# Own orders at the start and the end of a fused agent-attention and maxout kernel

## The chip, the cores and the metric

The kernel runs on one core of a Trainium2 chip. The metric is the device time of one execution in microseconds (us); less is better. The engines are TensorE (PE: matmuls and transposes), VectorE (DVE), ScalarE (ACT), GpSimd (POOL) and SyncE (SP), which issues the loads and stores.

## The reference

Two layers, one behind the other. `B, N, C = 4, 12544, 128`, 49 agents, 768 hidden features.

```python
def _attn_ref(q, k, v, agents):
    scale = 1.0 / np.sqrt(q.shape[-1])
    def sm(a, b):
        s = scale * (a @ b.transpose(0, 2, 1))
        s = s - s.max(-1, keepdims=True)
        e = np.exp(s)
        return e / (e.sum(-1, keepdims=True) + 1e-09)
    a2k = sm(agents, k)
    agent_v = a2k @ v
    q2a = sm(q, agents)
    return (q2a @ agent_v).astype(np.float32)

def _moe_ref(x, w1, w2, w3, w_out):            # x: the 50176 rows of the attention
    h = np.maximum(np.maximum(x @ w1, x @ w2), x @ w3)
    return (h @ w_out).astype(np.float32)
```

All inputs and the output are float32.

## The kernel before

The kernel never forms the attention's output. For each batch it reduces keys and values to a small matrix `avT` (agent values, 128 x 49), multiplies that with the difference of the weights (`wall`: w2-w1, w3-w1, and a linear part) into `G` (49 rows), and then each row of queries needs only its 49 exponentials `e` times `G`.

**Two kinds of groups.** A *key group* (`k_group`) covers 9 tiles of 128 rows: load, cast to bf16, transpose, scores against the agents, exponentials, values, add. Batch 0 is reduced by "early" key groups before any query; their rows are cut into ten groups of 9 tiles and two of 4, so the last one covers tiles 94 to 97. Batches 1 to 3 are reduced inside the query groups of the batch before. A *query group* (`q_group`, 49 of them, `s` = 0 to 48, 8 tiles each) loads and casts queries, transposes them on PE or by DMA, and makes scores and exponentials (`s`, `ex`). Then, for each of six slices `f` of the hidden features:

- `u<f>`: PE, the first hidden product (L533, two matmuls), into a PSUM tile of the ring "uv"
- `a<f>`: ScalarE, relu of it into SBUF (L548); for `f` = 3 in place (L545)
- `v<f>`: PE, the second hidden product (L533), into another tile of the ring "uv"; for `f` = 3 added to u3's tile
- `x<f>`: VectorE, the maximum of both into `r` (L558); for `f` = 3 ScalarE's relu (L556)
- `oc<o><f>`: PE, the output product of slice `f` for output half `o` (L572, four matmuls), added to the tile that `lin<o>` (L563) began
- `sc<o>`: scaling of output half `o` with the reciprocal row sums (L579); then one store of the group by SP

`sums` (PE, L521) and `rec` (VectorE, L527) make those reciprocals.

**Order by keys.** Every step is put down with `at(key, fn, name, needs, ring, frees)`, and `emit` sorts all steps by their key. A step whose `needs` have not been emitted, or whose PSUM ring has no free place, waits in a list and is emitted as soon as it can be. The rings are "uv" (3 tiles of two banks), "om" (2 tiles) and "a" (3 SBUF tiles of relu results). The emitted order is the order of each engine's own queue: each engine works strictly through it. `table(s)` chooses the keys of a query group: `KEY` for most, `BEGIN` and `BORDER` where a batch begins or is about to, `LATE` from group 36 on, the last batch, in which no keys are left to reduce.

**The seam.** `last_key` is the key of the last early key group. Around it stand that group's steps, the first query group's load, cast (POOL, L481), transposes (PE, L486), copy (ScalarE, L494), scores (L507) and exponentials, and the tail of batch 0's reduction (`k_tail`): `normalise` (L402, L403) makes `avT`, `product` (L421) multiplies it with `wall` in PSUM, and VectorE copies it into `G` (L426). For batch 0, `product` fills one "uv" tile in two parts, each copied out before the next begins, and then a second tile. All loads go through SP's queue into a ring of 14 SBUF tiles `st`; the early values are cast by ScalarE (L285), all keys and queries by POOL (L280, L481). Between the steps `keep_busy` puts a few matmuls without use (L254).

Of the kernel before, what the change touches and what calls it, by code (L numbers as in the profile page):

```python
# [16 lines left out]
def kernel(  # L17
# [78 lines left out]
        "oc11": 11.381, "oc13": 11.497,  # L96
    }
    PRODUCT_KEYS = (-8.717, -1.818)
    BEHIND = 2.6

    def table(s):
        if s + 1 in tails:
            return BORDER
        return BEGIN if s in tails and s < SB else KEY if s < SB else LATE
# [6 lines left out]
    def uv_tile(dtype=FP32):  # L111
        return psum.tile([P, 2, 512 if dtype == FP32 else 1024], dtype, tag="uv", bufs=3, name="uv_ps")
# [6 lines left out]
    def at(key, fn, name=None, needs=(), ring=None, frees=()):  # L119

        ops.append((key, len(ops), fn, name, needs, ring, frees))
# [61 lines left out]
    def load_tile():  # L185
        return loads.tile([P, KT, C], FP32, tag="st", name="st")
# [77 lines left out]
    def k_group(b, t0, n, key, s):  # L264
# [4 lines left out]
        if s == 0:  # L269
            key += BEHIND  # L270

        def load():
            for name, src in (("k", k), ("v", v)):
                t = d[name] = load_tile()
                nc.sync.dma_start(t[:, :n, :], src[b, t0 * P:(t0 + n) * P, :].rearrange(
                    "(p j) c -> p j c", j=n))
# [4 lines left out]

        def cast_v():
            d["vb"] = work.tile([P, KT, C], BF16, tag="v_bf", bufs=4, name="v_bf")
            if early:
                nc.scalar.activation(d["vb"][:, :n, :], d["v"][:, :n, :], AF.Copy)  # L285
            else:
                nc.gpsimd.tensor_copy(out=d["vb"][:, :n, :], in_=d["v"][:, :n, :])  # L287
# [59 lines left out]

        if early:
            g = ("early", t0)
            at(key - 30, load)  # L350
            at(key - 5, cast_k)
            at(key - 4, cast_v)
            at(key, turn_k, ("kt", g), (), "uv", [("kt_out", g)])
            at(key + 0.5, evacuate, ("kt_out", g), [("kt", g)])

            last = [("normalise", 0)] if t0 + n == NT else []
            late = max(0, (key - last_key) / 6 + 2)
            at(min(key + 6.6, last_key + 0.58 + 0.02 * late), scores, ("ks", g), [("kt_out", g)],
               "uv", [("ka", g)] + last)
            at(min(key + 7, last_key + 0.64 + 0.01 * late), exps, ("ke", g), [("ks", g)])  # L360
            done = last_key + (0.6 + 0.1 * late if late >= 1 else 0.55)
            at(min(key + 13.2, done), values, ("kv", g), [("ke", g)])
            at(min(key + 13.6, done + 0.01), add_values, ("ka", g), [("kv", g)])
        else:

            at(max(6.0 * s - 24.6, 6.0 * s - 21.05 if s in (4, 5) else -99), load)
            at(max(6.0 * s - 12.6, last_key - 3.4 + 0.2 * s), cast_k, ("k_cast", s))
            at(max(6.0 * s - 10.6, last_key - 3.3 + 0.2 * s), cast_v, ("v_cast", s))
            if s > 1:
                at(max(key - 9.1, last_key - 3.2), turn_k, ("kt_out", s), [("k_cast", s)])  # L370
            else:

                turn = 2.7 if s else last_key + 1.05
                at(turn, turn_k, ("kt", s), (), "uv", [("kt_out", s)])
                at(turn + 0.05, evacuate, ("kt_out", s), [("kt", s)])
            at(key + K["ks"], scores, ("ks", s), [("kt_out", s), ("ho", s)])
            at(key + K["ke"], exps, ("ke", s), [("ks", s)])
            at(key + K["ke"] + 1.5, add_exps, ("kx", s), [("ke", s)])
            at(key + K["kv"], values, ("kv", s), [("ke", s), ("v_cast", s)])
            at(key + K["ka"], add_values, ("ka", s), [("kv", s)])  # L380

    def k_tail(b, sum_key, keys, s):
        d = {}

        def reduce():
            w = KT // 2 * A
            t = Eacc[b]
            while w >= A:
                nc.gpsimd.tensor_tensor(out=t[:, :w], in0=t[:, :w], in1=t[:, w:2 * w], op=ALU.add)
                w = w // A // 2 * A  # L390
            nc.gpsimd.tensor_tensor(out=e_sum[:, :A], in0=t[:, :A], in1=t[:, KT * A - A:], op=ALU.add)

        def total():
            for h in range(2):
                nc.tensor.matmul(host[s][h * H:(h + 1) * H, :1], e_sum, ones[:, :1], start=True,
                                 stop=True, skip_group_check=True)

        def normalise():
            if s is None:

                r = last_tile["t"][:, :A]
                nc.vector.reciprocal(r, Vacc[b][:, A:])  # L402
                nc.vector.tensor_tensor(out=avT[:, b, :A], in0=Vacc[b][:, :A], in1=r, op=ALU.mult)  # L403
            else:
                nc.vector.reciprocal(r_ag[:, b:b + 1], host[s][:, :1])
            G[b] = work.tile([P, WC], BF16, tag="G", name="G")

        def product(c0, *ends):

            t = uv_tile().rearrange("p i c -> p (i c)")  # L410

            at0 = c0 if len(ends) == 1 else ends[0] - 512
            a = c0
            for z in ends:
                cuts = sorted({a, z} | {c for c in (at0 + 512, C1O) if a < c < z})
                for lo, hi in zip(cuts, cuts[1:]):
                    for h in range(2):


                        c = lo + (C if lo >= C1O and h == 0 else 0)  # L420
                        nc.tensor.matmul(t[h * H:(h + 1) * H, lo - at0:hi - at0], avT[:, b, :],  # L421
                                         wall[:, c:c + hi - lo], start=True, stop=True,
                                         skip_group_check=True)
                src = t[:, a - at0:z - at0]
                if s is None:
                    nc.vector.tensor_copy(out=G[b][:, a:z], in_=src)  # L426
                else:
                    nc.scalar.activation(G[b][:, a:z], src, AF.Copy, scale=r_ag[:, b:b + 1])
                a = z

        if s is not None:
            at(6.0 * (s - 1) + table(s - 1)["ke"] + 1.51, reduce, ("sum_e", b), [("kx", s - 1)])
            at(sum_key + 0.8, total, ("total", s), [("sum_e", b), ("ho", s)])
        at(sum_key + 0.81, normalise, ("normalise", b),
           [("ka", ("early", NT - last_size))] if s is None else [("total", s), ("ka", s - 1)])

        pieces = ((C31, C31 + 2 * P, C1O) if s is None else (C31, WC), (C21, C31))
        for i, piece in enumerate(pieces):
            at(keys[i], lambda piece=piece: product(*piece),
               ("product", b, i), [("normalise", b)], "uv", [("product", b, i)])  # L440


    def split(t0, t1, step):
# [10 lines left out]
    def q_group(s):  # L454
# [120 lines left out]
        def out_scale(o):  # L575
            if "out" not in d:
                d["out"] = work.tile([P, GT, C], FP32, tag="o_sb", bufs=3, name="o_sb")
            j, m = 2 * pairs[o][0], 2 * len(pairs[o])
            nc.vector.tensor_tensor(  # L579
                out=d["out"][:, j:j + m, :],  # L580
                in0=d["o", o].rearrange("p (j c) -> p j c", c=C),
                in1=d["r"][:, j:j + m].unsqueeze(2).to_broadcast([P, m, C]), op=ALU.mult)
# [14 lines left out]
        if s == 0:  # L597
            at(last_key - 29.9, load)
            at(last_key - 3.5, cast)
            at(last_key + 0.802, turn_q, ("qt", 0), (), "om", [("qe", 0)])  # L600
            at(last_key + 0.803, evacuate, ("qe", 0), [("qt", 0)])
            at(last_key + 0.94, scores, ("s", 0), [("qe", 0)], "om", [("ex", 0)])
            at(last_key + 0.941, exps, ("ex", 0), [("s", 0)])
        elif not q_dma:
            at(key - (21.08 if s in (4, 5) else 26), load)
            at(max(key - 12.8, last_key - 3.45 + 0.2 * s), cast, ("q_cast", s))
            put("qt", turn_q, ("q_cast", s), ring="om", frees=[("qe", s)])
            put("qe", evacuate, ("qt", s), *([("s", s - 3)] if s >= 3 else []))
        else:
            at(key - 32, load)  # L610
            at(key - 14.3, cast)
            at(key - 12.3, turn_q_dma, ("qe", s))
# [56 lines left out]
    for g, n in enumerate(first_sizes):  # L669
        k_group(0, sum(first_sizes[:g]), n, first_key + 6.0 * g, None)  # L670

        if 4 <= g < len(first_sizes) - 3:
            fillers += [(first_key + 6.0 * g + 0.55, 3), (first_key + 6.0 * g + 1.3, 3)]
    k_tail(0, last_key, (last_key + 0.95, last_key + 1.02), None)
    for key, n in fillers + [(last_key + 0.9, 2), (KEY["u1"] + 0.01, 2),
                             (KEY["u3"] + 0.05, 2)]:
        at(key, lambda n=n: keep_busy(n), ("busy", key), (), "om", [("busy", key)])
# [45 lines left out]
```

## Time and profile before

| | |
|---|---|
| time, median of 6 runs | 463.16 us (463.10 to 463.39) |
| the profiled execution's own time | 463.25 us |
| its span in the profile | 461.4 us, 13320 instructions |
| PE busy | 436.8 us (95%) |
| DVE busy | 402.3 us (87%) |
| ACT busy | 396.7 us (86%) |
| POOL busy | 171.4 us (37%) |
| DMA | 118.53 MB, mean 257 GB/s |
| granted TensorE clock | 1.00 |

The span runs from the first to the last instruction of the program; 1.85 us of the execution lie outside it. All times below are microseconds from the span's start. A busy share is a mean over stages that have different limits: until about 45 us the core mostly loads and reduces batch 0, then come 49 query groups, and behind the last one the output is scaled and stored. `DVE r L558` means an instruction of VectorE at line 558 of the kernel that writes the tile `r`.

### The profile page before, as it was taken

The page shows a single profiled execution, that of the slowest core. Times are in us where ns is not written, and L with a number is a line of the kernel's source. Part 1 is how long each engine was busy: PE and PEld are TensorE (multiplying, and loading weights), DVE is VectorE, ACT ScalarE, POOL GpSimd, SP SyncE. Part 2 cuts the span into 40 slices and gives each one's busy share as a digit, 9 for nine tenths or more (in the row PEclk, how much of TensorE's full clock was granted, in tenths as well). Part 3 has the DMA queues.
Part 4 walks back from the last instruction along what each step waited for, and adds up shares of the span by engine and source line. Part 5 has one row for each costly group of instructions (what it writes and reads, how often), then busy time and mean ns, then how long its engine had stood idle before and what let it go on. Part 6 is the DMA issues. An engine that isn't in the chain of part 4 may idle for free.

```text
span 461.4 us, 13320 instructions
## 1 busy us (share of the span) xinstructions
PE 436.8 (95%) x5457; PEld 273.9 (59%) x5462; DVE 402.3 (87%) x510; ACT 396.7 (86%) x460; POOL 171.4 (37%) x179
## 2 busy tenths in 40 slices
PE   2598899999999999999999999999999999999996
PEld 2465466666656666666666666666656555555554
DVE  3255899999989999999989999999988999999995
ACT  3365989999899899898998998999999999999982
POOL 2234964644462535445273355363240101100000
PEclk9999999999999999999999999999999999999999
DMA  8999999999998999987998999996766465644122
GB/s 316 408 409 391 352 325 353 333 345 263 312 305 284 305 267 342 283 268 246 301 317 277 280 316 304 284 266 188 162 149 183 127 195 151 180 118 125 60 94 91
DMA packets 82632, 118.53 MB, mean 257 GB/s; under 512 B 56391, under 2 KB 57867, under 8 KB 82571
## 3 DMA queue, kind: packets, MB, share of 16 engines
q1 hardware_dynamic: 82368, 117.59, 84.4%
q8 instruction: 42, 0.69, 0.6%
q14 instruction: 19, 0.16, 0.1%
q10 hardware_dynamic: 203, 0.10, 0.1%
HBM read 78.74 MB, written 25.69 MB: 226 GB/s over the span
## 4 chain that ended last, share of the span: by engine, by line
PE 80%; DMA 8%; DVE 5%; ACT 4%; issue 1%; SPq 0%; POOL 0%; DVEq 0%; ACTq 0%
PE uv_ps L533 34%; PE o_ps L572 29%; PE o_ps L563 6%; DMA st<-in_k_dram 5%; PE m_ps L486 4%; DVE r L558 4%; PE m_ps L507 3%; ACT a_sb L548 2%; DMA st<-in_q_dram 2%; DMA st<-in_v_dram 2%; PE m_ps L323 2%; PE m_ps L312 1%; PE m_ps L521 1%; DVE o_sb L579 0%; DVE G L426 0%
## 5 line engine op out<-in xcount | busy, mean ns | idle before, releaser
L558 DVE TENSOR_TENSOR r<-uv_ps,a_sb 128x1024 bf16<-128x1024 f32 x245 | 297.6, 1221 | 16.2 <-PE uv_ps L533 7.6
L548 ACT ACTIVATE a_sb<-uv_ps 128x1024 bf16<-128x1024 f32 x245 | 240.8, 1027 | 15.4 <-PE uv_ps L533 13.9
L533 PE MATMUL uv_ps<-e_q,G 49*128 49x512 bf16 (+3 forms) x1248 | 186.7, 368 | 2.6 <-DVE G L426 0.4
L572 PE MATMUL o_ps<-wo_bf,r 128*128 128x128 bf16 x2352 | 175.3, 220 | 0.2 <-DVE r L558 0.2
L572 PEld LDWEIGHTS <-r 128*128 128x128 bf16 x2352 | 137.8, 98 | 40.0 <-issue 38.0
L533 PEld LDWEIGHTS <-G 49*128 49x128 bf16 x1248 | 57.8, 93 | 64.6 <-issue 32.7
L342 POOL TENSOR_TENSOR Eacc<-Eacc,e_k 128x441 f32<-128x441 f32 (+1 forms) x30 | 30.4, 1015 | 124.0 <-ACT e_k L317 124.0
L579 DVE TENSOR_TENSOR o_sb<-o_ps,recips 128x512 f32<-128x512 f32 x98 | 67.5, 689 | 9.1 <-PE o_ps L572 6.3
L481 POOL CAST q_bf<-st 128x1024 bf16<-128x1024 f32 x49 | 50.9, 1040 | 62.2 <-DMA qT<-q_bf 59.1
L556 ACT ACTIVATE r<-uv_ps 128x1024 bf16<-128x1024 f32 x49 | 50.2, 1024 | 18.0 <-PE uv_ps L533 17.7
L280 POOL CAST k_bf<-st 128x1152 bf16<-128x1152 f32 (+2 forms) x45 | 50.2, 1117 | 29.9 <-DMA st<-in_k_dram 27.0
L545 ACT ACTIVATE uv_ps<-uv_ps 128x1024 f32<-128x1024 f32 x49 | 49.6, 1012 | 0.2
L563 PE MATMUL o_ps<-G,e_q 128*128 128x256 bf16 x196 | 38.0, 276 | 0.0
L287 POOL CAST v_bf<-st 128x1152 bf16<-128x1152 f32 (+1 forms) x33 | 37.4, 1135 | 0.7 <-ACT e_q L513 0.3
L513 ACT ACTIVATE e_q<-m_ps 128x512 bf16<-128x512 f32 x49 | 29.8, 609 | 0.5 <-PE m_ps L507 0.5
L285 ACT ACTIVATE v_bf<-st 128x1152 bf16<-128x1152 f32 (+1 forms) x12 | 12.9, 1073 | 14.0 <-DMA st<-in_v_dram 14.0
L563 PEld LDWEIGHTS <-e_q 128*128 128x128 bf16 x196 | 12.5, 97 | 18.7 <-issue 18.0
L300 DVE COPY kT<-uv_ps 128x1152 bf16<-128x1152 bf16 (+1 forms) x14 | 9.9, 709 | 14.8 <-PE uv_ps L294 14.8
L486 PEld LDWEIGHTS <-q_bf 128*128 128x128 bf16 x264 | 14.9, 98 | 12.9 <-issue 11.1
L492 DVE COPY qT<-m_ps 128x1024 bf16<-128x1024 bf16 x32 | 21.8, 681 | 0.0
L486 PE MATMUL m_ps<-ident,q_bf 128*128 128x128 bf16 x264 | 20.4, 220 | 0.3 <-POOL q_bf L481 0.3
L507 PE MATMUL m_ps<-qT,agT 128*64 128x512 bf16 (+3 forms) x104 | 19.9, 388 | 0.7 <-ACT qT L494 0.7
(71 smaller groups left out, 225.7 us busy)
## 6 DMA issues: line engine op xcount, KB each, us to landing
st<-in_q_dram SPq DMA_DIRECT2D x46, 512.0 KB, 4.8
out_dram<-o_sb SPq DMA_DIRECT2D x46, 512.0 KB, 3.8
st<-in_k_dram SPq DMA_DIRECT2D x40, 576.0 KB, 6.8
st<-in_v_dram SPq DMA_DIRECT2D x40, 576.0 KB, 7.6
st<-in_k_dram SPq DMA_DIRECT2D x3, 512.0 KB, 7.4
st<-in_v_dram SPq DMA_DIRECT2D x3, 512.0 KB, 6.5
wst<-in_moe_w_dram SPq DMA_DIRECT2D x3, 384.0 KB, 10.5
st<-in_q_dram SPq DMA_DIRECT2D x2, 384.0 KB, 4.8
```

The source lines that it names most:

```text
L280: nc.gpsimd.tensor_copy(out=d["kb"][:, :n, :], in_=d["k"][:, :n, :])
L287: nc.gpsimd.tensor_copy(out=d["vb"][:, :n, :], in_=d["v"][:, :n, :])
L481: nc.gpsimd.tensor_copy(out=d["qb"], in_=d["q"])
L486: nc.tensor.transpose(t[:, j * P:(j + 1) * P], d["qb"][:, j, :], ident)
L533: nc.tensor.matmul(t[:, h, j0 * P:j1 * P], G[b][h * H:h * H + A, col + f * P:col + (f + 1) * P], d["e"][h * H:h * H + A, j0 * P:j1 * P], s ...
L545: nc.scalar.activation(u, u, AF.Relu)
L548: nc.scalar.activation(a_sb[f], u, AF.Relu)
L556: nc.scalar.activation(r, v_ps[f], AF.Relu)
L558: nc.vector.tensor_tensor(out=r, in0=v_ps[f], in1=a_sb[f], op=ALU.max)
L563: nc.tensor.matmul(t[:, i * 2 * C:(i + 1) * 2 * C], d["e"][:, jj * P:(jj + 1) * P], G[batch[jj]][:, C1O:C1O + 2 * C], start=(i == 0), stop ...
L572: nc.tensor.matmul(t[:, c:c + C], r_sb[f][:, h, jj * P:(jj + 1) * P], wo_bf[:, f, :], start=False, stop=True, skip_group_check=True)
L579: nc.vector.tensor_tensor(out=d["out"][:, j:j + m, :], in0=d["o", o].rearrange("p (j c) -> p j c", c=C), in1=d["r"][:, j:j + m].unsqueeze( ...
```

## The change

It has three parts.

1. *Loads and the last early values.* The last early key group's load is split: its keys keep their place, its values are loaded behind the first queries. Their cast goes from ScalarE to VectorE, with another key.
2. *The seam's order.* The first queries' transposes and their copy get keys that are a little smaller. Batch 0's product is cut into three steps. The first fills the first half of one "uv" tile (256 columns, which u0 and u1 need) and is copied; the second fills another tile (512 columns of the third weights' part and 512 of the second's), copied in two pieces; the third puts the remaining 256 columns into the other half of the first tile. The key of the first two lies ahead of the first queries' scores, the third's behind them.
3. *The last four groups.* Query groups 45 to 48 get a table of keys each (`LAST`). In group 48, output half 1 is scaled by four ScalarE instructions of 128 columns instead of one VectorE instruction of 512.

```diff
     def table(s):
+        if s >= NQ - len(LAST):
+            return LAST[s - NQ]
         if s + 1 in tails:
             return BORDER
...
-        def load():
+        def load(names="kv"):
             for name, src in (("k", k), ("v", v)):
+                if name not in names:
+                    continue
...
         def cast_v():
-            if early:
+            if early and t0 + n == NT:
+                nc.vector.tensor_copy(out=d["vb"][:, :n, :], in_=d["v"][:, :n, :])
+            elif early:
                 nc.scalar.activation(d["vb"][:, :n, :], d["v"][:, :n, :], AF.Copy)
...
-            at(key - 30, load)
+            last = t0 + n == NT
+            at(key - 30, lambda: load("k" if last else "kv"))
+            if last:
+                at(key - 29.87, lambda: load("v"))
             at(key - 5, cast_k)
-            at(key - 4, cast_v)
+            at(key + 0.645 if last else key - 4, cast_v)
...
+        cut = C31 + 2 * P
+        def product_first():
+            t = d["p"] = uv_tile().rearrange("p i c -> p (i c)")
+            multiply(t, 0, C31, cut)
+            nc.vector.tensor_copy(out=G[b][:, C31:cut], in_=t[:, :cut - C31])
+        def product_second():
+            t = uv_tile().rearrange("p i c -> p (i c)")
+            multiply(t, 0, cut, C1O)
+            multiply(t, 512, C21, C21 + 512)
+            nc.vector.tensor_copy(out=G[b][:, cut:C1O], in_=t[:, :C1O - cut])
+            nc.vector.tensor_copy(out=G[b][:, C21:C21 + 512], in_=t[:, 512:])
+        def product_third():
+            multiply(d["p"], 512, C21 + 512, C31)
+            nc.vector.tensor_copy(out=G[b][:, C21 + 512:C31], in_=d["p"][:, 512:512 + C31 - C21 - 512])
...
-        pieces = ((C31, C31 + 2 * P, C1O) if s is None else (C31, WC), (C21, C31))
-        for i, piece in enumerate(pieces):
-            at(keys[i], lambda piece=piece: product(*piece),
-               ("product", b, i), [("normalise", b)], "uv", [("product", b, i)])
+        if s is None:
+            at(keys[0], product_first, ("product", 0, 0), [("normalise", 0)], "uv", [("product", 0, 2)])
+            at(keys[0] + 0.001, product_second, ("product", 0, 1), [("product", 0, 0)], "uv",
+               [("product", 0, 1)])
+            at(keys[1], product_third, ("product", 0, 2), [("product", 0, 0)])
+        else:
+            for i, piece in enumerate(((C31, WC), (C21, C31))):
+                at(keys[i], lambda piece=piece: product(*piece), ("product", b, i), [("normalise", b)],
+                   "uv", [("product", b, i)])
...
         def out_scale(o):
+            if s == NQ - 1 and o == 1:
+                for i in range(m):
+                    nc.scalar.activation(d["out"][:, j + i, :], d["o", o][:, i * C:(i + 1) * C], AF.Copy,
+                                         scale=d["r"][:, j + i:j + i + 1])
+                return
...
-            at(last_key + 0.802, turn_q, ("qt", 0), (), "om", [("qe", 0)])
-            at(last_key + 0.803, evacuate, ("qe", 0), [("qt", 0)])
+            at(last_key + 0.76, turn_q, ("qt", 0), (), "om", [("qe", 0)])
+            at(last_key + 0.77, evacuate, ("qe", 0), [("qt", 0)])
             at(last_key + 0.94, scores, ("s", 0), [("qe", 0)], "om", [("ex", 0)])
...
-    k_tail(0, last_key, (last_key + 0.95, last_key + 1.02), None)
+    k_tail(0, last_key, (last_key + 0.93, last_key + 1.02), None)
```

`multiply` holds the matmul loop that was inside `product`. Sorted by their keys, the steps that PE takes from u1 of group 48 on are, with the group behind each name that is not 48's:

```
before: u1 | oc04.46 oc05.46 | u2 | oc03.46 | v0 u3 | lin1.47 oc10.47 oc14.47 | v2 v3 v1 |
        oc15.47 oc13.47 oc12.47 oc11.47 | u4 u5 | lin0.47 oc02.47 | v4 | oc01.47 oc00.47 | v5 |
        oc04.47 oc05.47 oc03.47 lin1 oc10 oc14 oc15 oc13 oc12 oc11 lin0 oc02 oc01 oc00 oc04 oc05 oc03
after:  u1 | oc03.46 oc05.46 oc00.46 | u2 v1 u3 | lin1.47 oc15.47 oc10.47 oc12.47 oc14.47 |
        v0 v2 v3 | oc11.47 oc13.47 lin0.47 oc03.47 oc02.47 | u4 v4 | oc00.47 oc05.47 oc01.47 | u5 v5 |
        oc04.47 lin1 oc13 oc11 oc12 oc10 oc14 lin0 oc04 oc03 oc00 oc01 oc15 oc05 oc02
```

The bars mark each change between hidden products and the others. In VectorE's order of group 48, x1 x0 x2 stand in place of x0 x2 x1, and the scaling of half 0 of group 47 goes ahead of x5.

## The prediction

> **What bounds the kernel now.** I read the page first: TensorE (PE) is busy for 95% of the span, and the chain that ended last runs through PE for 80% of it. In the middle a group costs PE 7.83 of its 7.86 us (windows from 421.63 to 445.22), so time can only be found at the two ends. The chain of waits over the first 75 us came next. Columns: start, length, what.
>
> ```profile
> 32.28 8.36 DMA st<-in_q_dram
> 40.70 1.05 POOL q_bf L481
> 41.79 0.64 PE m_ps L486 x8
> 42.45 1.03 ACT qT L494
> 43.52 0.41 PE m_ps L507 x2
> 43.93 0.12 PE uv_ps L421 x2
> 44.08 0.44 DVE G L426
> 44.55 0.42 PE uv_ps L421 x2
> 45.00 1.56 DVE G L426 x2
> 46.61 0.39 PE uv_ps L533 x2
> ```
>
> Until 40.64 the chain waits for the first queries; then the product (L421) stands behind the scores (L507), though avT was ready at 42.79. The second batch of L421 waits 0.5 us for the copy out of the same PSUM tile, and u1 (46.61) waits for the last copy. The end of the chain:
>
> ```profile
> 445.64 1.24 DVE r L558
> ...
> 447.88 1.03 ACT uv_ps L545
> 448.91 0.04 issue
> 448.95 0.61 PE uv_ps L533 x4
> ...
> 453.22 1.22 DVE r L558
> 454.44 0.05 issue
> 454.49 1.07 PE o_ps L572 x16
> 455.56 0.22 PE o_ps L563 x2
> 455.77 1.35 PE o_ps L572 x24
> 457.13 0.02 issue
> 457.15 0.69 DVE o_sb L579
> ```
>
> PE waits here for x5 of group 47, for a3 and for x5 of group 48, and 42 matmuls still stand behind the last x5. Last, the timeline of the first 10 us, for the price of the cast that moves to VectorE: one line of each engine, answered one engine at a time.
>
> ```profile
> 5.51 1.18 DVE L206 CAST ag_bf<-ag_st 49x512 bf16<-49x512 f32 x1 [3.21 <-DMA ag_st<-in_agents_dram]
> ```
> ```profile
> 5.28 1.14 POOL L280 CAST k_bf<-st 128x1152 bf16<-128x1152 f32 x1 [3.97 <-DMA st<-in_k_dram]
> ```
>
> A VectorE cast of 512 f32 elements a row, begun while a POOL cast ran, ended at 6.69, 0.27 us after POOL's 6.42.
>
> **The start, step by step.** (1) *Loads.* Single transfers land in order of issue: last keys 38.67, last values (256 KB) 39.34, queries (512 KB) 40.64. With the queries ahead: 38.67+1.30 = 39.97, and the values at 40.64. SP issues the same loads; the bytes ahead of the output weights (41.94) and of group 0's keys (43.69) are the same.
> (2) *Queries.* POOL's cast, 1.04 us, runs from 40.03 to 41.07. PE's 8 transposes issue at 41.12 to 41.57; ScalarE's copy (1.03) ends at 42.83, before 43.48.
> (3) *Last values' cast.* ScalarE loses 0.62 us (39.38 to 40.00), worth nothing: its next instruction waits for PE until 40.54. VectorE could begin at 40.70, beside POOL's cast. Bounds from L206: 0.27 from its own start (40.97), or 1.18 (41.88). I take the row's pattern, 0.27 behind POOL: 41.34. Behind it on VectorE stands the add of the group before (ready at 41.3), which nobody awaits sooner. PE cannot begin these values before 41.6 anyway, since the queries' transposes now stand ahead of them: the cast costs 0, at most 0.3.
> [...]
> (4) *avT.* The values' matmuls (0.35 as at 41.16) end at 41.95. From the last add's start to avT took 1.01 (41.78 to 42.79): 42.00+1.01 = 43.01, 0.22 later than before.
> (5) *Product.* It no longer waits for the scores: PE 43.05 instead of 43.74, first copy 43.39 instead of 44.08. The second part has its own tile, so copies follow back to back: 0.42, then 512, 512 and 256 wide at 0.65, 0.65 and 0.42, ending at 45.5 instead of 46.56. That is one copy more (+0.16), less the 0.5 wait, less 0.69.
> (6) *What is late next.* The scores stand behind six product matmuls, so the exponentials end at 44.65 instead of 44.57; nobody is waiting, because PE next needs group 0's keys, which POOL casts until 44.99 as before. Transposes 45.03, and u0 follows 0.61 later as before: 45.64 instead of 45.83. So ScalarE, back to back from a0 on, gains 0.19. u1 comes 0.8 earlier and x0 (47.97) about 0.85, so v3 no longer stands behind v1's wait: x3 (49.92) gains 0.45, and with it its PSUM buffer, the transposes at 50.99, and a4 (52.02). From there to 58.23 ScalarE runs back to back and PE takes over, so 0.45 should stay. The low end is 0, or -0.2 if the queries land no sooner; the high end adds 0.35 that ScalarE idles before 59.08 without a releaser I can name. I take **0.4**.
>
> **The end, step by step.** From chain and timeline, a hidden step (two L533) costs 0.22, an output step (four L572) 0.22, a linear step (two L563) 0.22, and each change between L533 and the others 0.10 more (x2 0.32, x4 0.54). From u1 of group 48 at 445.22, both orders hold 11 hidden, 27 output and 4 linear steps: 2.42+6.02+0.88 = 9.3. Sorted by its keys, the old order has 13 changes, 1.37: 10.7. The last L572 ended at 457.13, of which 0.16 is latency, so PE waited 1.05: 0.18 for x5 of 47 (446.92), 0.50 for a3 (448.95), 0.37 for x5 of 48 (454.49).
> New order: 9 changes (saves 0.42). v3 stands three steps further behind u3: 0.50 gone. Output steps on x5 come last, three in all: 0.37 gone. v1 now comes third behind v5 of 47 in the ring of three tiles and takes its buffer, so it waits for x5 of 47, which ended at 446.87: 0.38 where 0.18 was. Sum: 0.42+0.50+0.37-0.20 = **1.1**.
> Does x5 of 48 come in time? On VectorE, from v0 at 448.67: x0 449.10, x2 450.24, the scaling of 47 451.37, x4 452.15 (after a4), scaling 453.25, x5 453.87 to 455.08. PE reaches it at 455.17. The slack is 0.1, and every further delay costs its own size. PE ends at 456.0, the last VectorE scaling at 456.7, against 457.84.
> The other half's four ScalarE scalings, 128 wide: the nearest row is 0.27 (L240, 128x128); L249 (128x256) took 0.40. Four are 0.8 to 1.6, from 455.6: done at 456.4 to 457.2. I take 0.27 each, hidden beside VectorE's; the other end costs 0.5. The last store takes its 2.61 us from issue to landing as before.
> Groups 45 to 47 are nearly unmoved: exponentials one step (1.02) later against 2.4 of slack (441.24 to 443.65), reciprocals behind x5 in two groups (1.2 later, 0.87 before PE needs their buffer), two changes more in one group (0.21, inside PE's waits of 0.36 per group). Cost 0 to 0.2; I take 0. Bounds of the end: 0.4 to 1.4.
>
> **Sum.** The profiled execution took 463.25 (span 461.4, 1.85 around it): 463.25-0.4-1.1 = 461.75. The median before is 0.09 lower, 463.16, which makes 461.66; I say **461.7**, 0.3% less. This kernel's measurement can tell about 0.2% (0.93 us) from no change.
>
> **Rivals.**
> *Tail only:* u0 gains 0.19, and what follows is bound by something that lands at its old time (group 1's keys 47.82, queries 50.54). Against it: those casts end before PE asks. 463.16-1.1 = 462.05, between 461.8 and 462.4.
> *Start only:* x5 of 48 is 0.5 or more later than reckoned, or ScalarE's scalings take 0.40 each, and the end gives back 0.7 to 1.1. For it: slack of 0.1 alone. 462.75.
> *Slower: TensorE falls back to half clock at the seam.* L294's transposes were 104 ns apart until 21.97 and 56 from 25.58 on, so a slower pace exists, though the granted clock reads 1.00 in both windows. Once fast, gaps of 0.68 and 0.52 us (42.84, 44.04) left it fast. The new order leaves about 0.9 twice, 42.2 to 43.05 and 44.1 to 45.0. If the pace halves there it needs some 4 us of work to come back (21.14 to 25.58), 3.1 of them busy: 463.16-1.1+3.1 = 465.2. The point from which it decides lies above 0.68; gaps of 1.3 us at 8.17 and 11.04 occurred only while it was slow.
> [...]
>
> **How the numbers follow.** Both ends as reckoned: 0.62 (461.0 to 462.2). Tail only: 0.15. Start only: 0.14. Slower: 0.09. Faster by over 0.2% (under 462.23) is the first and three quarters of the second: 0.73; the same is the rest of the second and the third: 0.18; slower 0.09. The range runs from 460.9 to 463.0; it leaves out the slower case and the far ends.
>
> **What would show it.** Right: the first query cast near 40.0; VectorE's values cast ending about 0.27 after it; L421 before L507 near 43.05; the last G copy near 45.5; a4 of group 0 near 51.6; from u1 of 48 to the last scaling's end 11.5 instead of 12.6 us; no PE wait of over 0.1 before the last output steps. Wrong: the query cast still at 40.7, transposes 104 ns apart after 44, PE waiting for x5 at the end, or last scalings on ScalarE that end well after VectorE's.

## The result and the profile after

The changed kernel took 462.02 us (median of 16 runs, 461.69 to 462.45) against 463.26 (median of 34, 463.10 to 463.40): a ratio of 0.9974, 95% interval 0.9967 to 0.9980. It is faster by 1.24 us where 1.5 were forecast. The profiled execution took 461.92, its span is 460.1. Lines of the kernel after are used from here on: the product is L464, scores L572, hidden products L598, maxima L623, scalings L650 and L647.

**The seam.** In these timelines the columns are start, length, line, operation, tiles, and in brackets the idle time before it with its releaser.

```profile
40.06 1.04 POOL L546 CAST q_bf<-st 128x1024 bf16<-128x1024 f32 x1 [0.61 <-DMA st<-in_q_dram]
```
```profile
40.75 0.63 DVE L327 CAST v_bf<-st 128x512 bf16<-128x512 f32 x1
...
42.88 0.21 DVE L451 TENSOR_TENSOR avT<-Vacc,uv_ps 128x49 bf16<-128x49 f32 x1
43.49 0.42 DVE L479 CAST G<-uv_ps 128x256 bf16<-128x256 f32 x1 [0.40 <-PE uv_ps L464]
43.92 0.69 DVE L485 CAST G<-uv_ps 128x512 bf16<-128x512 f32 x1
44.52 0.68 DVE L486 CAST G<-uv_ps 128x512 bf16<-128x512 f32 x1
45.12 0.42 DVE L490 CAST G<-uv_ps 128x256 bf16<-128x256 f32 x1
```

The queries are cast 0.64 us earlier, VectorE's cast of the last values ends at 41.38, 0.28 behind GpSimd's 41.10, and the four copies into `G` stand back to back up to 45.54, where the last ended at 46.56 before. The chain of waits no longer goes through them:

```profile
35.28 8.30 DMA st<-in_k_dram
...
43.73 1.16 POOL k_bf L322
44.89 0.05 issue
44.94 0.68 PE uv_ps L338 x9
45.61 0.54 PE uv_ps L598 x4
```

The load of group 0's keys (landing at 43.59), their cast and their transposes now lead to u0 (45.54).

**The end.** The chain from x5 of group 47 on, and ScalarE's last row:

```profile
445.29 1.24 DVE r L623
446.52 0.04 issue
446.56 0.61 PE uv_ps L598 x4
...
454.22 1.58 PE o_ps L637 x28
455.79 0.02 issue
455.82 0.69 DVE o_sb L650
```
```profile
455.37 1.14 ACT L647 ACTIVATE o_sb<-o_ps,recips 128x128 f32<-128x128 f32 x4 [2.19 <-PE o_ps L637]
```

PE waits once, for x5 of group 47 (v1 starts at 446.56), and then no more up to the last output step. ScalarE's four scalings start 0.25 apart, 0.37 long, and end with VectorE's last, at 456.51. From u1 of group 48 (444.86) to there it is 11.65 us, where it was 12.62.

**Where the lead came from and where it went.** ScalarE's in-place relu (a3) runs once in each query group. How much earlier it starts than in the kernel before, from both traces:

| group | 0 | 1 | 2 to 15 | 16 to 38 | 39 | 40 to 47 | 48 | last scaling's end |
|---|---|---|---|---|---|---|---|---|
| lead, us | 0.37 | 0.63 | 0.93 | 0.72 | 0.42 | 0.35 | 0.08 | 1.33 |

The start won 0.93 at group 2, more than twice what was forecast; 0.30 of it comes at once between groups 1 and 2. Three steps of 0.2 to 0.36, at groups 16, 39 and 48, took 0.85 of it back. The orders of groups 1, 2, 16 and 39 are the same in both kernels.

### The profile page after: what moved, and what is told of

The parts are those of the page before. It is cut to its first block, busy times and chain, and to the rows that moved or that the text cites. A ratio compares the mean times of both kernels' runs of the same rounds, so it can differ in the third digit from the quotient of the medians.

```text
span 460.1 us, 13325 instructions
## 1 busy us (share of the span) xinstructions
PE 436.5 (95%) x5457; PEld 273.9 (60%) x5462; DVE 401.7 (87%) x511; ACT 397.1 (86%) x463; POOL 171.5 (37%) x179
## 4 chain that ended last, share of the span: by engine, by line
PE 80%; DMA 9%; DVE 5%; ACT 3%; issue 2%; SPq 1%; POOL 0%; ACTq 0%; POOLq 0%; DVEq 0%
PE uv_ps L598 34%; PE o_ps L637 29%; DMA st<-in_k_dram 7%; PE o_ps L628 6%; DVE r L623 4%; PE m_ps L551 4%; PE m_ps L572 3%; ACT a_sb L613 2%; DMA st<-in_v_dram 2%; PE m_ps L367 1%; PE m_ps L356 1%; PE m_ps L586 1%; SPq L317 1%; DVE o_sb L650 0%; ACT e_q L578 0%
## 5 line engine op out<-in xcount | busy, mean ns | idle before, releaser
L623 DVE TENSOR_TENSOR r<-uv_ps,a_sb 128x1024 bf16<-128x1024 f32 x245 | 297.5, 1220 | 17.0 <-PE uv_ps L598 8.1
L598 PE MATMUL uv_ps<-e_q,G 49*128 49x512 bf16 (+3 forms) x1248 | 186.8, 368 | 2.1 <-DVE r L623 0.6
L598 PEld LDWEIGHTS <-G 49*128 49x128 bf16 x1248 | 57.9, 93 | 64.6 <-issue 32.7
L650 DVE TENSOR_TENSOR o_sb<-o_ps,recips 128x512 f32<-128x512 f32 x97 | 66.8, 689 | 8.3 <-PE o_ps L637 5.7
L572 PE MATMUL m_ps<-qT,agT 128*64 128x512 bf16 (+3 forms) x104 | 19.9, 388 | 0.0
```

What stands on the lines that cost most here:

```text
L598: nc.tensor.matmul(t[:, h, j0 * P:j1 * P], G[b][h * H:h * H + A, col + f * P:col + (f + 1) * P], d["e"][h * H:h * H + A, j0 * P:j1 * P], s ...
L623: nc.vector.tensor_tensor(out=r, in0=v_ps[f], in1=a_sb[f], op=ALU.max)
L650: nc.vector.tensor_tensor(out=d["out"][:, j:j + m, :], in0=d["o", o].rearrange("p (j c) -> p j c", c=C), in1=d["r"][:, j:j + m].unsqueeze( ...
```

## Experiments: the two ends apart

All times below are medians, with the ratio to runs of the kernel before on the same chip. Their medians are 463.26 for the four kernels of this section; 463.33 for the three with shifted memsets in the next one and for the old product; 463.24 for the merged memsets, the cast on ScalarE and group 48 alone; 463.28 for the last kernel. "Lead" is used as in the table above, and the lead at the end is that of the last scaling's end.

**Start only.** The four new orders are not used, and half 1 of group 48 is scaled by VectorE again.

```diff
-        if s >= NQ - len(LAST):
-            return LAST[s - NQ]
...
-            if s == NQ - 1 and o == 1:
+            if False:
```

> The changed start, the old order of the last four groups, and the last scaling on VectorE as before. Theory 'two gains': in the profile the start is 0.93 us ahead from group 2 on; some of that is taken back on the way by single stalls (0.22 at group 16 and 0.36 at group 39 in the profiled run of the changed kernel), so 0.35 to 0.93 us remain at the end: 462.3 to 462.9. Rival 'the end alone': what the start wins is absorbed by TensorE's tight middle, 463.0 to 463.3.

Measured: 462.88 (462.76 to 463.30), ratio 0.9993 [0.9984, 1.0002]. The lead is 1.01 at group 2, 0.78 from 16 on, 0.41 from 40 on, and 0.49 at 48 and at the last scaling. The start alone wins 1.0 and loses over half of it on the way, with no change at the end: the losses at groups 16 and 39 do not come from the new orders.

**End only.** Loads, casts, product and keys of the seam as before.

> The old start, the new order of the last four groups and the ScalarE scaling. Theory 'two gains': from u1 of group 48 to the last scaling's end 11.65 us instead of 12.62, so 0.9 to 1.05 us less than before: 462.2 to 462.4, and groups 0 to 44 lie at their times of before within 0.05 us. Rival 'the end alone': the whole 1.24 us, 462.0. If the new order also needs the start's phase, less than 0.7 us is gained.

Measured: 461.84 (461.74 to 461.95), ratio 0.9968 [0.9956, 0.9981]. The lead is 0.00 up to group 44, 0.21 at 48 and 1.44 at the last scaling. So the end alone is worth more than the whole change. PE waits nowhere from 445 to 456 in this trace: the wait for x5 of group 47 isn't there.

**Scaling of the last half on VectorE.** Everything else as changed.

```diff
-            if s == NQ - 1 and o == 1:
+            if False:
```

> The changed kernel, but output half 1 of group 48 is scaled by one VectorE instruction as before. Theory: it would run from 455.4 to 456.1 by the changed kernel's profile and hold up the scaling of half 0, which began at 455.82, by 0.2 to 0.3 us: 462.2 to 462.3. Rival: the four ScalarE instructions (each 0.37, ending at 456.51, together with VectorE) are themselves what ends last, and nothing or 0.1 us is lost.

Measured: 462.33 (461.89 to 462.48), ratio 0.9978 [0.9968, 0.9987]. From a3 of group 48 to the last scaling it wins 1.10, where the changed kernel wins 1.25: ScalarE's scalings are worth 0.15 in the trace and 0.3 in the medians.

**The old order of loads, and ScalarE's cast.**

```diff
-            if early and t0 + n == NT:
-                nc.vector.tensor_copy(out=d["vb"][:, :n, :], in_=d["v"][:, :n, :])
-            elif early:
+            if early:
...
-            at(key - 30, lambda: load("k" if last else "kv"))
-            if last:
-                at(key - 29.87, lambda: load("v"))
+            at(key - 30, load)
...
-            at(key + 0.645 if last else key - 4, cast_v)
+            at(key - 4, cast_v)
```

> The changed kernel, but the last values are loaded ahead of the first queries and cast on ScalarE as before; the new product and all new orders stay. Theory: the queries land at 40.64 instead of 40.01, the transposes (which now stand ahead of the last values on TensorE) begin at 41.8 instead of 41.16 and push avT and all copies into G by 0.6: u0 near 46.1 instead of 45.54, 0.4 to 0.6 us lost: 462.4 to 462.6. Rival 'keys bind': group 0's keys, cast until 44.9, set u0 anyway, and under 0.2 us is lost.

Measured: 461.89 (461.80 to 462.01), ratio 0.9969 [0.9958, 0.9981]. The lead is 0.30 from group 2, 0.16 from 8, 0.00 from 23 on, 0.21 at 48 and 1.45 at the end. So the new product alone, without the new loads, leads by 0.30; how the rest divides is taken up further down. But this kernel is no slower than the changed one, and it loses at two other places, groups 8 and 23. The losses hang neither on the moment nor on the groups.

## Experiments: every 128th instruction of VectorE

Counting VectorE's rows in the trace from 0 (semaphore rows too), each of the losses at groups 8, 16, 23 and 39 falls on a row whose number is 63 more than a multiple of 128. Which instruction stands there, and the gap between its row and the one before it:

| row | before | changed | old loads |
|---|---|---|---|
| 191 | semaphore | semaphore | a maximum (L619): 0.42, the loss at group 8 |
| 319 | semaphore | a maximum (L623): 0.19, the loss at group 16 | copy of queries: none |
| 447 | semaphore | semaphore | a maximum: 0.40, the loss at group 23 |
| 575 | scaling: 0.10 | a maximum: 0.40, but no loss | semaphore |
| 703 | reciprocals | a maximum: 0.40, the loss at group 39 | semaphore |
| 831 | x5 of group 47: 0.40 | x5 of group 47: 0.39, as before | scaling: none |

Of the changed kernel's 245 maxima, 135 start 0.04 behind the semaphore row ahead of them. The gaps of 0.39 to 0.42 stand right behind a semaphore row too; where a maximum runs right up to the row (the scalings and the copy) the gap is 0.10 or none. The change has one cast and one copy more at the start, so all that follows stands two rows later; with the old loads it is one. In the kernel with the new end alone, x5 of group 47 stands on row 829 with a gap of 0.04, and PE's wait for it is gone. The new theory was: VectorE stands still for some 0.3 us at every 128th instruction, which costs time only where the instruction there was ready and something waits for it. Four runs tested it in both directions.

```diff
-    nc.vector.memset(ones, 1.0)
+    nc.gpsimd.memset(ones, 1.0)
...
-    nc.vector.memset(e_sum[:, A:], 1.0)
+    nc.gpsimd.memset(e_sum[:, A:], 1.0)
```

> The changed kernel with two of VectorE's first memsets (ones, and the tail of e_sum) given to GpSimd, which is idle then: nothing else differs, but everything that VectorE runs later stands two places earlier in its stream, where the kernel with only the four new orders had it. New theory (VectorE stands still for 0.2 to 0.4 us at every 128th instruction of its stream, and what that costs hangs on which instruction falls there): the lead over the kernel before stays 0.93 from group 2 to group 44, the 0.36 wait ahead of the last relu of group 47 is gone, and the time is 463.26 - 0.93 - 1.42 = 460.9. Rival one (the losses at groups 16 and 39 hang on the moment, on a transfer or on the buffers, not on the count of instructions): they stay, 462.0. Rival two (the two parts' gains meet at a wait that both would have removed): the lead stays 0.93 in the middle and is given back in the last group, 462.0.

Measured: 461.39 (461.13 to 461.76), ratio 0.9960 [0.9947, 0.9972]. The steps at groups 16 and 39 and the wait for x5 of group 47 are gone. The lead is 0.70 at group 2, drifts to 0.60 by group 40 (no run shows why), is 0.66 at 48 and 1.91 at the end. The theory's mechanism held; its number, 460.9, missed by 0.5: the lead began at 0.70, and 2.06 to 2.16 us lay around the spans of its runs, where the changed kernel has 1.74 to 1.85.

The kernel before, made to look like the changed one:

```diff
-    nc.vector.memset(busy, 1.0)
+    for c in range(0, 512, 172):
+        nc.vector.memset(busy[:, c:min(c + 172, 512)], 1.0)
```

> The kernel before with one of VectorE's first memsets (busy) made in three pieces in place of one, at 1.05 us, when VectorE has nothing to do until 5.5 us: nothing else differs, but everything after it stands two places later in VectorE's stream. Theory of the 128th instructions: against the kernel before it falls behind by 0.2 at group 16 and by 0.3 more at group 39, where the shifted stream has a relu on the 128th place, and wins back about 0.1 at group 48, where the place leaves the last relu of group 47: 463.26 + 0.4 = 463.7. Rivals: 463.26, no step at any group.

Measured: 463.55 (463.35 to 463.75), ratio 1.0004 [0.9996, 1.0013]. In the trace it falls behind by 0.22 at group 16 and by 0.36 more at groups 39 and 40, and wins 0.35 back at group 48: the changed kernel's losses at 16 and 39, made by two more memsets at 1 us. In time this is 0.22, which the interval doesn't separate from nothing; the steps in the trace do.

Start only, with the two memsets on GpSimd:

> The start's part alone (no orders of their own for the last four groups, the last outputs scaled by VectorE) with the same two memsets on GpSimd. Theory of the 128th instructions: the lead of 1.0 at group 2 stays through group 44, where without the shift it was 0.41, and the time is 463.26 - 0.95 = 462.3. Rivals: as without the shift, 462.9, the lead down by 0.23 at group 16 and by 0.30 at group 39.

Measured: 463.21 (463.03 to 464.51), ratio 1.0000 [0.9991, 1.0009]. The lead is 0.81 at group 2 and still 0.81 at group 47, as the theory said; at group 48 it falls by 0.28 to 0.53. VectorE's row 831 can't be the reason: x5 of group 47 stands there in the kernel before too, and still starts 0.81 earlier here (444.83 against 445.64). The relu behind it is late, on ScalarE; see below. In time the forecast missed by 0.9: around the spans lie 2.08 to 2.17 us again, 0.33 more than without the GpSimd memsets, the lead began 0.2 lower, and the 0.28 at group 48 had been left out of the forecast.

The two memsets are better merged on VectorE than moved:

```diff
-    busy = const.tile([P, 512], BF16, name="busy")
-    nc.vector.memset(busy, 1.0)
-    ones_bf = const.tile([P, P], BF16, name="ones_bf")
-    nc.vector.memset(ones_bf, 1.0)
+    lot = const.tile([P, 512 + P], BF16, name="busy_ones")
+    nc.vector.memset(lot, 1.0)
+    busy, ones_bf = lot[:, :512], lot[:, 512:]
-    agT = const.tile([P, B, H], BF16, name="agT")
-    nc.vector.memset(agT, 0.0)
...
-    avT = const.tile([P, B, H], BF16, name="avT")
-    nc.vector.memset(avT, 0.0)
+    two = const.tile([P, 2, B, H], BF16, name="agT_avT")
+    nc.vector.memset(two, 0.0)
+    agT, avT = two[:, 0], two[:, 1]
```

> The changed kernel with four of VectorE's first memsets made as two (busy with ones_bf in one tile, agT with avT in another): two instructions fewer at the head of VectorE's stream, and nothing more on GpSimd. With the memsets on GpSimd the steps at groups 16 and 39 were gone, but the lead at group 2 was 0.70 where the changed kernel has 0.93, group 0's keys were cast 0.23 later, and 2.11 us lay around the span where others have 1.8. Theory: both of these came with GpSimd's two memsets; here the lead is 0.93 from group 2 through group 44, 1.8 lie around the span, and the time is 463.26 - 0.93 - 1.42 = 460.9. Rival: the 0.23 is the price of the shift itself (the 128th place falls on other instructions at the seam): lead 0.70, time 461.1.

Measured: 461.22 (461.00 to 462.56), ratio 0.9962 [0.9950, 0.9975]. The lead is 0.74 from group 2 to group 47, without a step, and 2.06 at the end; 1.76 to 1.82 lie around the spans. So the GpSimd memsets explain what lay around the span, but not the lower lead at the start. VectorE's timeline at the loss of group 39, of the changed kernel, then of this one, then of the kernel before with two more memsets:

```profile
371.84 0.68 DVE L650 TENSOR_TENSOR o_sb<-o_ps,recips 128x512 f32<-128x512 f32 x1
372.82 1.22 DVE L623 TENSOR_TENSOR r<-uv_ps,a_sb 128x1024 bf16<-128x1024 f32 x1 [0.31 <-PE uv_ps L598]
```
```profile
371.80 0.68 DVE L648 TENSOR_TENSOR o_sb<-o_ps,recips 128x512 f32<-128x512 f32 x1
372.44 1.23 DVE L621 TENSOR_TENSOR r<-uv_ps,a_sb 128x1024 bf16<-128x1024 f32 x1
```
```profile
372.83 0.68 DVE L580 TENSOR_TENSOR o_sb<-o_ps,recips 128x512 f32<-128x512 f32 x1
373.82 1.23 DVE L559 TENSOR_TENSOR r<-uv_ps,a_sb 128x1024 bf16<-128x1024 f32 x1 [0.31 <-PE uv_ps L534]
```

The scaling and the maximum behind it are the same in all three. The maximum follows at once where it stands on row 701, and 0.31 after the scaling's end where it stands on row 703. The releaser that is named had nothing to do with it: the semaphore row ahead of the changed kernel's maximum was over at 372.43. At such places the profile has packets of instructions; for 372 to 375 of the changed kernel, and then for its whole span, the list of DMA queues has (packets, MB, share):

```profile
q8 instruction: 1, 0.02, 2.3%
q14 instruction: 1, 0.01, 0.9%
```
```profile
q8 instruction: 42, 0.69, 0.6%
q14 instruction: 19, 0.16, 0.1%
```

In the trace q14's packet has 8192 bytes; if there is one for every 128 rows, that is 64 bytes a row, an estimate. The 19 of the span are as many as there are rows 63 above a multiple of 128 on VectorE (7), ScalarE (7), SyncE (3) and GpSimd (2). q8's 42 packets have 16384 bytes each, and PE and its weight loads have 10929 rows. q14's packet starts 0.7 us after the maximum that was held up (373.53 against 372.82), here and at groups 16 and 47, so the maximum didn't wait for these bytes; what held it up, no run shows. What was measured is its length: where nothing covered it, VectorE idled for 0.19 us ahead of row 319, 0.31 ahead of row 703 and 0.36 ahead of row 831 of the changed kernel, and the lead lost 0.22 at group 16 and 0.36 at 39 and 40.

**ScalarE has such rows too.** Counted the same way, ScalarE's rows 63 and 831 hold a relu in some of the kernels. For row 63 it is the relu of `f` = 3 in group 1; the kernel before, then the changed one:

```profile
59.08 1.02 ACT L556 ACTIVATE r<-uv_ps 128x1024 bf16<-128x1024 f32 x1 [0.84 <-PE uv_ps L533]
```
```profile
58.14 1.02 ACT L621 ACTIVATE r<-uv_ps 128x1024 bf16<-128x1024 f32 x1 [0.54 <-PE uv_ps L598]
```

Before, it stands on row 63, 0.35 behind the semaphore row ahead of it; in the changed kernel on row 62, 0.04 behind. The cast that went to VectorE has left ScalarE's stream one instruction shorter there. For row 831 it is the relu a2 of group 48, which waits for x5 of group 47: in the changed kernel it begins 0.32 behind its semaphore row, before, on row 832, 0.04. The traces side by side, with the rows of these two, the row of x5 of group 47 on VectorE, and what the lead gains from one group to the next:

| kernel | relu of group 1 | lead, 1 to 2 | a2 of 48 | x5 of 47 | lead, 47 to 48 |
|---|---|---|---|---|---|
| before | 63 | - | 832 | 831 | - |
| start only, GpSimd memsets | 62 | +0.30 | 831 | 831 | -0.28 |
| start only | 62 | +0.31 | 831 | 833 | +0.07 |
| before, two more memsets | 63 | 0.00 | 832 | 833 | +0.35 |
| changed | 62 | +0.30 | 831 | 831 | -0.28 |
| merged memsets | 62 | +0.31 | 831 | 829 | +0.07 |
| end only | 63 | 0.00 | 832 | 829 | +0.21 |
| old loads | 63 | 0.00 | 832 | 830 | +0.21 |

So 0.30 of the start's lead is this relu leaving row 63. In the last group, with the old orders (the first four lines), a2 on ScalarE's row 831 costs 0.28 and x5 on VectorE's costs 0.35, each with or without the other; with the new orders (the last four) they cost 0.14 and 0.35. From group 47 to the last scaling the new end wins 0.98 with both, 1.32 with a2's alone and 1.45 with neither, which is why the end alone beat the whole change. No run moved ScalarE's rows on purpose, so this rests on the comparison of traces; the other kernels with the same orders fit it to 0.03.

## Experiments: what bounds the seam

The same start gave leads from 0.36 to 1.11 at group 2. The profiles tell why: group 0's keys land at different moments, though nothing ahead of them in SP's queue differs.

| kernel | keys land | u0 | lead at group 2 |
|---|---|---|---|
| last half scaled by VectorE | 43.41 | 45.37 | 1.11 |
| start only | 43.52 | 45.48 | 1.01 |
| changed | 43.59 | 45.54 | 0.94 |
| start only, GpSimd memsets | 43.71 | 45.67 | 0.81 |
| memsets merged | 43.77 | 45.73 | 0.75 |
| changed, GpSimd memsets | 43.81 | 45.77 | 0.70 |
| group 48 alone (further down) | 44.16 | 46.12 | 0.36 |
| kernel before | 43.69 | 45.83 | 0 |

In the seven kernels with the new start u0 comes 1.95 to 1.96 after the keys, and landing and lead add up to 44.51 to 44.53. Before, it was 2.14. The seam is bound by this load now, and every comparison of leads has to allow for its landing.

**The old product, with the new loads**, and with the memset of `ones` on GpSimd. The main lines of the edit:

```diff
...
+        pieces = ((C31, C31 + 2 * P, C1O) if s is None else (C31, WC), (C21, C31))
+        for i, piece in enumerate(pieces):
+            at(keys[i], lambda piece=piece: product(*piece),
+               ("product", b, i), [("normalise", b)], "uv", [("product", b, i)])
...
-    k_tail(0, last_key, (last_key + 0.93, last_key + 1.02), None)
+    k_tail(0, last_key, (last_key + 0.95, last_key + 1.02), None)
```

> The changed kernel with the first product as before (one tile, key 0.95, behind the first scores), and one memset (ones) on GpSimd, so that VectorE's stream stands as in the shifted kernel; the new order of the loads, VectorE's cast and the end stay. Old loads with the new product led by 0.30 at group 2, all together by 0.93. If the two add, this leads by 0.63 at group 2 and keeps it through group 44: 463.26 - 0.63 - 1.42 = 461.2. If the product behind the scores takes back what the loads bring (its copies end at 46.55 as before), it leads by 0.0 to 0.2 at group 2: 461.7.

Measured: 461.36 (461.19 to 462.70), ratio 0.9963 [0.9950, 0.9975]; the lead is 0.65 from group 2 to 47. Its keys landed at 43.65, which allows 0.87, so the old product costs 0.22. By the same reckoning (keys at 43.64, 0.88 allowed, 0.30 had), the kernel with the old loads lacks 0.58. But 0.30 of it is ScalarE's row 63, since that kernel also casts on ScalarE again; 0.28 are left for the loads. At the landing of the kernel before, 43.69, the new start would lead by 0.83: about 0.22 from the product, 0.28 from the loads and 0.30 from ScalarE's row.

**The last values' cast on ScalarE**, in the new place, with `agT` and `avT` cleared by one memset.

```diff
-                nc.vector.tensor_copy(out=d["vb"][:, :n, :], in_=d["v"][:, :n, :])
+                nc.scalar.activation(d["vb"][:, :n, :], d["v"][:, :n, :], AF.Copy)
```

> The changed kernel with the last values cast by ScalarE as before, in the new place, and two memsets made as one (agT with avT), so that VectorE's stream is again two places shorter. My prediction put the price of VectorE's cast beside GpSimd's at 0, since TensorE comes to these values only after the queries' transposes: then this runs as the kernel with four memsets made as two, a lead of 0.93 at group 2, 460.9. Rival: the cast that waits for GpSimd's holds up the adds behind it and so avT: then avT comes 0.1 to 0.3 earlier here, and the time is 460.6 to 460.8. Other rival: the cast on ScalarE pushes back the copy of the queries, 461.2.

Measured: 461.66 (461.38 to 462.33), ratio 0.9968 [0.9956, 0.9980], 0.44 behind the kernel with merged memsets. ScalarE's timeline:

```profile
40.69 0.63 ACT L326 ACTIVATE v_bf<-st 128x512 bf16<-128x512 f32 x1 [1.34 <-PE uv_ps L355]
41.23 0.54 ACT L360 ACTIVATE e_k<-uv_ps 128x196 bf16<-128x196 f32 x2
42.44 1.02 ACT L558 ACTIVATE qT<-m_ps 128x1024 bf16<-128x1024 bf16 x1 [0.67 <-PE m_ps L550]
```

The cast stands ahead of the last exponentials of the key groups (41.23, in the changed kernel 40.56), and they hold up the values' products: `avT` is ready at 43.71 instead of 43.09. Neither rival had named these exponentials. Yet the later `avT` explains little of the time. The lead is 0.27 at groups 1 and 2, where the kernel with merged memsets has 0.44 and 0.75. The 0.17 at group 1 is the keys' landing (43.95 against 43.77; u0 follows 1.96 behind, at 45.91, as elsewhere), and the other 0.30 come from the cast back in ScalarE's stream, with the relu of group 1 on row 63 again. That VectorE's cast is worth something at the seam itself isn't shown; what its move won here is ScalarE's row.

**An own order for group 48 alone**, on the kernel with merged memsets.

```diff
-        if s >= NQ - len(LAST):
+        if s == NQ - 1:
```

> As the kernel with four memsets made as two, but with an order of its own for group 48 alone; groups 45 to 47 keep the old one. My prediction put the orders of groups 45 to 47 at 0 to 0.2 of cost and no gain: then this takes 460.9, or up to 0.2 less. Rival: the order of group 47 is what frees TensorE of its waits at the start of group 48, and without it 0.3 to 0.5 come back: 461.2 to 461.4.

Measured: 468.84 (468.41 to 470.27), ratio 1.0126 [1.0112, 1.0140]. All expectations missed. The waits of PE from 440 to 468 (in total, times, longest):

```profile
PE uv_ps L596 <- DVE r L621: 2.1, 2, 1.6
PE o_ps L626 <- DVE o_sb L648: 1.7, 2, 1.2
```

Group 48's order reckons with the output steps of group 47, which group 47's own order puts off. With the old order of group 47 they have been used up, and PE waits for VectorE and ScalarE: that is read from the orders and the waits, and no further run tests it. The four orders are one plan: group 48's without the other three costs 7.6 us.

**The seam's two bounds moved together**, with `agT` and `avT` cleared by one memset.

```diff
-    at(last_key - 29.85, load_w_out)
+    at(-24.59, load_w_out)
...
-            nc.vector.tensor_copy(out=G[b][:, C21 + 512:C31], in_=d["p"][:, 512:512 + C31 - C21 - 512])
+            nc.scalar.activation(G[b][:, C21 + 512:C31], d["p"][:, 512:512 + C31 - C21 - 512], AF.Copy)
```

> The changed kernel with agT and avT cleared by one memset, and two edits at the seam: the output weights are loaded behind group 0's keys and values in place of ahead of them, and the last copy of the first product (256 wide, 45.25 to 45.67 on VectorE) is made by ScalarE, which is idle from 44.86 to 46.17 (this too takes one instruction from VectorE's stream, two in all, as in the kernel with four memsets made as two, which led by 0.74 at group 2 and took 461.22). There u0 starts at 45.74: the keys, landing at 43.77, let the transposes before it start at 45.13, and the buffer that u0 takes is free when the last copy ends, 45.67, so moving one of the two alone wins nothing. Theory (these two bound the seam): keys land near 42.5, the copy ends near 45.3, u0 starts near 45.35, the lead grows by 0.4 to 1.1, and the time is 460.8. Rival one: what comes next in group 0 (the queries of group 1, whose cast stands behind both, or the key transposes of group 1) takes over, and the lead stays at 0.75: 461.2. Rival two: the 128th place of VectorE's stream now falls on the copy of group 0's turned keys and holds it by 0.3, which holds the scores: the lead is 0.75 or less.

Measured: 460.47 (460.44 to 461.03), ratio 0.9945 [0.9931, 0.9958], the fastest of all, 1.55 below the changed kernel. The chain at the seam:

```profile
43.02 0.73 PE uv_ps L463 x6
43.75 0.23 PE m_ps L571 x2
...
44.50 0.39 ACT G L489
44.88 0.04 issue
44.93 0.61 PE uv_ps L597 x4
```

The keys landed at 41.97 and left the chain; the last copy into `G`, on ScalarE, is over at 44.88 and u0 starts at 44.93. The lead is 1.34 from group 2 to 47 without a step, and 2.79 at the end. It won more than expected, since u0 came 0.4 earlier than reckoned; and from group 47 to the end it wins 1.45, where the kernel with merged memsets wins 1.32, as a2 of group 48 stands on ScalarE's row 833. Which of the two edits at the seam is worth how much isn't shown, since both were made together.

## Why the prediction was right, step by step

**Start, steps 1 to 5: right to a tenth.** Queries landed at 40.01 (39.97 forecast), the last values at 40.73 (40.64), VectorE's cast ended at 41.38 (41.34), `avT` was ready at 43.09 (43.01), the product came ahead of the scores at 43.14 (43.05), the last copy ended at 45.54 (45.5). The cast took 0.63 beside GpSimd's and ended 0.28 behind it, where 0.27 was taken over from the cast at L206, which took 1.18 beside another of GpSimd's. No run shows this cast alone.

**Step 6: mis-sized.** u0 gained 0.29 (0.19), x0 0.85 (0.85). I took 0.45 of lead to stay; 0.94 did, at group 2. The keys landed 0.10 sooner, and of the idle time ahead of 59.08, whose releaser I could not name and which I had left to the high end, 0.30 went away (0.84 became 0.54; that relu begins at 58.14): 0.45 + 0.30 + 0.10 = 0.85. This idle time was ScalarE's row 63, and the cast's move, booked at nothing on ScalarE, took the relu off it.

**What failed is a sentence of the first part**, that time can only be found at the two ends. It can be lost in the middle: 0.22 at group 16 and 0.36 at 39 and 40, because two more VectorE instructions at the start moved maxima to the 128th places. The start's net at group 47 is therefore 0.35, and the 0.4 that was forecast came out by luck, from two errors of opposite sign.

**End: the mechanism right, the term 0.1 too large.** 0.98 was won from group 47 on, for 1.1. The waits for a3 and for x5 of 48 went, x5 of 48 ended at 454.86 (455.08), and v1 waits for x5 of 47, as forecast. But x5 of 47 was late by VectorE's row 831 in both kernels, which I took for a fixed end (446.87), and a2 of 48 now fell on ScalarE's. The end alone, and the kernels whose rows are shifted, win 1.3 to 1.45 there. ScalarE's scalings, 0.37 each and 0.25 apart, took 1.14 (1.08). In the working of the end, 6.02 and 1.37 need 0.223 an output step and 0.105 a change, where the text has 0.22 and 0.10; the waits are read from the rows and don't hang on it.

**The rivals.** "Tail only" had its mechanism, something that lands at its old time: it is group 0's keys, but they leave 0.94. "Start only" fell: PE waits for nothing after 446.56. "Slower" fell too (its 3.1 is PE's busy time from 44 to 48; from 21.14 to 25.58 PE is busy for 4.22): the gaps were 0.73 and 0.68, and behind the one at 44.26 to 44.94 nine transposes took 0.68, where the slow pace of 104 ns would need 0.94; the granted clock reads 1.00 from 44 to 48. Whether a longer gap would slow PE down, no run shows.

## What to carry to other kernels

Before a lead at one end is booked for the whole kernel, compare the start of one repeated instruction in every stage, before and after: steps show where it is won and lost. A fraction of a microsecond hung here on which instruction stood at a fixed count in an engine's stream (0.22 us at group 16, 0.36 at 39 and 40), and an edit that moves work from one engine to another shifts both streams, so measure an edit with one or two harmless instructions more or fewer before you judge it, and merge such instructions rather than hand them to another engine (461.22 us against 461.39 here). When a seam has been shortened, look for the load that bounds it now, and move what isn't needed yet behind it; orders that were planned together are changed together.

## What was not expected of the hardware

- VectorE stood still ahead of maxima on rows 63 above a multiple of 128: 0.19 to 0.36 us where nothing covered it. What it waited for isn't settled.
- ScalarE's rows at the same count: 0.14 to 0.30 us, read from the comparison of traces; no run was made for it.
- Two memsets more on GpSimd at the start put 0.33 us around the span (2.06 to 2.17 against 1.73 to 1.86); one put none (1.78 to 1.86). Left open.
- Group 0's keys landed between 43.41 and 44.16 behind the same queue. The changed kernel's runs spread over 0.76 us, those before over 0.30; that the keys are the cause of the spread is likely, since only the new seam waits for them, but it is only argued.
